# Block-local attention and a three-way maximum layer: transposes moved from TensorE to VectorE and a DRAM scratch, one time table for all engines

## The chip, the core and the metric

The kernel runs on one core of a Trainium2 chip. The core has TensorE (PE, matrix products into PSUM; PEld is its weight load), VectorE (DVE), ScalarE (ACT), GpSimd (POOL) and SyncE (SP), which issues the transfers. Each engine takes its own instructions strictly in order and waits on semaphores for the others. The metric is the device time of one launch in microseconds (us), lower is better.

## The reference

Attention inside chunks of 64 positions, for 8 batches of 8 heads of 576 positions with 64 columns; its output, as 4608 rows of 512, goes through three products with 512x768 weights, their maximum, and one product with a 768x512 weight. All in float32.

```python
scores = scale * np.matmul(q_c, k_c.transpose(0, 1, 2, 4, 3))   # chunks of 64
scores = scores - np.max(scores, axis=-1, keepdims=True)
attn = np.exp(scores)
attn = attn / (np.sum(attn, axis=-1, keepdims=True) + 1e-09)
out = np.matmul(attn, v_c)
x = np.ascontiguousarray(out.transpose(0, 2, 1, 3)).reshape(B * S, H * D)
h = np.maximum(np.maximum(x @ w1, x @ w2), x @ w3)
return (h @ w_out).astype(np.float32)
```

## The kernel before

The 4608 rows are 36 tiles of 128 rows (two chunks of 64 positions, all heads), in nine groups of four tiles.

**Layer.** For a group, `hidden(j, w)` forms one 128x512 piece of x·w1, x·w2 or x·w3 (six `j`, three `w`), and `project` the four output tiles. Every float32 operand is kept as a high part (float32r) and a low part, the rest; `three` adds three products (low·high, high·low, high·high). A group has 72 such threes in `hidden` and 24 in `project`, 96 in all, 24 for each tile.

**Attention.** It makes the x of a later group while the layer of the present group runs. There are two forms. `plain_steps` (tiles below `PLAIN`) multiplies in plain float32, one product per head. `attention` ("stacked") puts high and low part in the two halves of the partitions: `qs` (q), `kk` (k), `vs` (v) and `aa` (the transposed softmax). For a stacked tile TensorE runs: a product of four matmuls for chunk 0 (called s0 here) and chunk 1 (s1), the transposes (`tp`), then the products with v for chunk 0 (x0) and chunk 1 (x1). After each product ACT copies one half out of PSUM and DVE adds the other. After s1 comes the softmax: DVE maximum, POOL subtraction, ACT exponential, DVE sum and reciprocal, POOL multiplication. After the transposes ACT and DVE split the result into `aa`, and two transfers inside SBUF, of 64 partitions each, copy each half of `aa` to the other 64 partitions. After x1, ACT writes the high part `xh` and POOL the low part `xl` of the group's x. The low parts of `qs`, `kk` and `vs` are POOL's too.

**Order.** Up to the eighth tile and the first group's layer the order of all engines is written out by hand (`FIRST`). Behind that only TensorE's order is set by hand: `due` gives each step of a tile a time, and `STEP`, the length of one three, is the clock by which steps are put between the threes. The other engines' instructions are ordered by the framework's scheduler. `now` counts the threes.

The buffers named here (`raw`, `qs`, `kk`, `aa`, `rv`, and the PSUM tiles s, tp and x) exist once each; `pm`, the layer's PSUM tiles, three times.

Of the kernel before, what the change touches and what calls it, by code (L numbers as in the profile page):

```python
# [19 lines left out]
P = 128  # L20
# [5 lines left out]
PLAIN = 10  # L26
# [20 lines left out]
F51f Y63 Y64 B65 A65 P01i F52f C65 hh5f D65 hl5f X65 xl7 H65 Y65p P01z P2z FP01 P3z FP2 FP3  # L47
# [4 lines left out]
def chunk_attn_maxout_kernel(  # L52
# [18 lines left out]
    ep = ctx.enter_context(tc.tile_pool(name="ep", bufs=2))  # L71
# [4 lines left out]
    ao_p = ctx.enter_context(tc.tile_pool(name="ao_p", bufs=1))  # L76
    ps_s = ctx.enter_context(tc.tile_pool(name="ps_s", bufs=1, space=PSUM))
# [88 lines left out]
    def softmax(e):  # L166
        mx = tmp.tile([P, 8], F32, name="mx")
        nc.vector.tensor_reduce(out=mx, in_=e, axis=AX.X, op=ALU.max)
        nc.gpsimd.tensor_tensor(out=e, in0=e, in1=mx.unsqueeze(2).broadcast_to([P, 8, 64]), op=ALU.subtract)
        nc.scalar.activation(out=e, in_=e, func=AF.Exp, scale=SCALE)  # L170
        run(over_sum(e))

    def run(steps):
        for s in steps:
            s()

    def plain_steps(t, x_of, col):
# [23 lines left out]
        def less():  # L201
            st["e"] = ep.tile([P, 8, 64], F32, name="e")
            nc.vector.tensor_tensor(out=st["e"], in0=st["s"],
                                    in1=st["mx"].unsqueeze(2).broadcast_to([P, 8, 64]), op=ALU.subtract)
# [37 lines left out]
    def plain_attention(t, x_of, col):  # L242
        ops = plain_steps(t, x_of, col)
        return [lambda names=names: run(ops[n] for n in names.split())
                for names in ("q v S mx sub exp sum eps rec nrm", "T at", "V xh xl")]

    halves_of = [slice(0, 64), slice(64, 128)]

    def attention(t, x_of, col):

        st = {}

        def stack(hi, src):
            nc.scalar.copy(out=hi, in_=src)  # L256
            nc.gpsimd.tensor_tensor(out=hi[64:], in0=src[64:], in1=hi[64:].bitcast(F32), op=ALU.subtract)  # L257

        def products(pool, name, c, lhs, rhs, out):
            o = pool.tile([P, 4, 2, 2, 64], F32, name=name)  # L260
            for g in range(4):
                nc.tensor.matmul(out=o[:, g].rearrange("p a h x -> p (a h x)"), lhsT=lhs[:, c, g, :],  # L262
                                 rhs=rhs[:, c, g].rearrange("p a x -> p (a x)"), start=True, stop=True)
            for h, rows in enumerate(halves_of):
                nc.scalar.copy(out=out[rows], in_=o[rows, :, 0, h, :])  # L265
            for h, rows in enumerate(halves_of):
                nc.vector.tensor_tensor(out=out[rows], in0=o[rows, :, 1, h, :], in1=out[rows], op=ALU.add)  # L267

        def operands():
            r = att.tile([P, 2, 2, 4, P], F32, name="r", tag="raw", bufs=1)  # L270
            nc.sync.dma_start(out=r, in_=qk2[t - PLAIN])
            rv = att.tile([P, 2, 4, P], F32, name="rv", tag="rv", bufs=1)
            nc.sync.dma_start(out=rv, in_=v2[t - PLAIN])
            qs = att.tile([P, 2, 4, P], F32R, name="qs", tag="qs", bufs=1)
            stack(qs, r[:, 0])
            kk = att.tile([P, 2, 4, 2, P], F32R, name="kk", tag="kk", bufs=1)
            for c in range(2):
                split(kk[:, c, :, 0, :], kk[:, c, :, 1, :], r[:, 1, c], nc.gpsimd)
            st.update(rv=rv, qs=qs, kk=kk)

        def scores(c):
            if c == 0:
                st["e"] = ep.tile([P, 4, 2, 64], F32, name="e")
            products(ps_s, "s", c, st["qs"], st["kk"], st["e"][:, :, c, :])
            if c == 1:
                ef = st["e"].rearrange("p g c k -> p (g c) k")
                softmax(ef)
                vs = st["vs"] = att.tile([P, 2, 4, P], F32R, name="vs", tag=f"vs{t % 2}", bufs=1)
                stack(vs, st["rv"])

        def transpose():
            tp = ps_t.tile([P, 4, P], F32, name="tp")
            for g in range(4):
                nc.tensor.transpose(out=tp[:, g, :], in_=st["e"][:, g].rearrange("p c k -> p (c k)"), identity=ident)  # L294
# [9 lines left out]
        def values(c):  # L304
            if c == 0:
                st["xs"] = xs_p.tile([P, 4, P], F32, name="xs")
            products(ps_x, "x", c, st["vs"], st["aa"], st["xs"][:, :, c * 64:(c + 1) * 64])
            if c == 1:
                xh, xl = x_of()
                split(xh[:, :, col:col + P], xl[:, :, col:col + P], st["xs"], nc.gpsimd)  # L310

        return [operands, lambda: scores(0), lambda: scores(1), transpose, lambda: values(0), lambda: values(1)]
# [3 lines left out]
    def moe(t0, x_of):  # L316
# [5 lines left out]
        def products(j, w, lo, hi):  # L322
            n, cols = hi - lo, slice(lo, hi)
            xh, xl = x_of()
            ps[j, w] = ps_m.tile([P, 512], F32, name="pm")
            for ct in range(CT):
                if ct:
                    yield
                three(ps[j, w][:, :n], wh[j][:, w, ct, :], wl[j][:, w, ct, :], xh[:, ct, cols], xl[:, ct, cols],
                      ct == 0, ct == CT - 1)  # L330

# [18 lines left out]
        def hidden(j, w):  # L350
            yield from products(j, w, 0, 512)
            maximum(j, w, 0, 512)
            if w == 2:
                high(j, 0, 512)
                low(j, 0, 512)

# [12 lines left out]
        def project(*tts):  # L369

            for js in (range(JT - 1), [JT - 1]):
                for tt in tts:
                    for j in js:
                        if (tt, j) != (tts[0], 0):
                            yield
                        onto(tt, j)
                    if JT - 1 in js:
                        output(tt)

        return dict(products=products, maximum=maximum, high=high, low=low, hidden=hidden, onto=onto,  # L380
                    output=output, project=project)

# [6 lines left out]

    def steps_of(i):  # L390
        return [(plain_attention if starts[i] + tt < PLAIN else attention)(starts[i] + tt, lambda: x_tiles(i), tt * P)
                for tt in range(GROUPS[i])]
# [19 lines left out]
    ops["P01i"] = lambda: [g0["onto"](tt, j) for tt in (0, 1) for j in range(JT - 1)]  # L412
    ops["P01z"] = lambda: [g0["onto"](tt, JT - 1) for tt in (0, 1)]
    ops["FP01"] = lambda: [g0["output"](tt) for tt in (0, 1)]
    for tt in (2, 3):
        ops[f"P{tt}z"] = lambda tt=tt: [g0["onto"](tt, j) for j in range(JT)]
        ops[f"FP{tt}"] = lambda tt=tt: g0["output"](tt)

# [20 lines left out]
    STEP = 0.681  # L439
    LENGTH = (3 * JT * CT + 4 * JT) * STEP  # L440

    def due(t):
        g, k = divmod(t, 4)
        if t < PLAIN:
            at = [(k - 4) * 13.0 - 11.0 + d for d in (0.0, 8.0, 13.0)]
        else:
            at = [(k - 4) * LENGTH / 4 - 19.0 + d for d in (-8.0, 0.0, 2.9, 16.5, 25.0, 28.2)]
        return [(g - 1) * LENGTH + a for a in at]

    events = sorted(((at, t, fn) for i in range(2, len(GROUPS)) for tt, u in enumerate(steps_of(i))  # L450
                     for t in [starts[i] + tt] for at, fn in zip(due(t), u)), key=lambda e: e[:2])
    now = 0.0
    with tc.manual_schedule(engines={mybir.EngineType.PE}):
        for i in range(1, len(GROUPS)):
            g = moe(starts[i], lambda i=i: x_tiles(i))
            for part in ([g["hidden"](j, w) for j in range(JT) for w in range(3)]
                         + [g["project"](0, 1), g["project"](2), g["project"](3)]):
                while True:
                    while events and events[0][0] <= now:
                        events.pop(0)[2]()  # L460
                    now += STEP
                    if next(part, part) is part:
                        break
# [41 lines left out]
```

## Time and profile before

| | |
|---|---|
| median of 3 runs | 714.3 us (712.72 to 714.6) |
| the profiled execution | 713.1 us, of which 711.4 us is the span of the instructions |
| TensorE busy | 703.1 us, 99% of the span |
| DVE, ACT, POOL busy | 398.9, 359.8 and 308.9 us |
| transfers | 38.5% of the 16 DMA engines' span, all issued by SP |
| granted TensorE clock | 1.000 |

All rows of the profile and of the trace are of this one execution. A row of the time line gives start, duration, engine, line, operation and tiles (out<-in); an idle stretch before it and who ended it stand in brackets.

### The profile page before, as it was taken

The page shows a single profiled execution, that of the slowest core. Times are in us where ns is not written, and L with a number is a line of the kernel's source. Part 1 is how long each engine was busy: PE and PEld are TensorE (multiplying, and loading weights), DVE is VectorE, ACT ScalarE, POOL GpSimd, SP SyncE. Part 2 cuts the span into 40 slices and gives each one's busy share as a digit, 9 for nine tenths or more (in the row PEclk, how much of TensorE's full clock was granted, in tenths as well). Part 3 has the DMA queues.
Part 4 walks back from the last instruction along what each step waited for, and adds up shares of the span by engine and source line. Part 5 has one row for each costly group of instructions (what it writes and reads, how often), then busy time and mean ns, then how long its engine had stood idle before and what let it go on. Part 6 is the DMA issues. An engine that isn't in the chain of part 4 may idle for free.

```text
span 711.4 us, 9743 instructions
## 1 busy us (share of the span) xinstructions
PE 703.1 (99%) x3545; PEld 592.9 (83%) x3546; DVE 398.9 (56%) x677; ACT 359.8 (51%) x665; POOL 308.9 (43%) x207
## 2 busy tenths in 40 slices
PE   8999999999999999999999999999999999999997
PEld 5997888888888888888888888888888888888886
DVE  7989852456456655676466637664566456521220
ACT  6675551445555555555555555556555655331111
POOL 2443020245656665555665555555566656100000
PEclk9999999999999999999999999999999999999999
DMA  9975640233433354333523363335333541120001
GB/s 365 410 275 185 195 139 31 88 117 114 149 124 119 111 144 131 119 118 84 184 90 118 119 177 119 119 120 171 120 105 107 160 134 33 30 75 15 1 1 59
DMA packets 23215, 90.28 MB, mean 127 GB/s; under 512 B 2944, under 2 KB 2944, under 8 KB 19840
## 3 DMA queue, kind: packets, MB, share of 16 engines
q1 hardware_dynamic: 23168, 89.67, 38.5%
q8 instruction: 28, 0.46, 0.3%
q14 instruction: 19, 0.16, 0.1%
HBM read 66.58 MB, written 9.44 MB: 107 GB/s over the span
## 4 chain that ended last, share of the span: by engine, by line
PE 95%; DMA 2%; DVE 1%; issue 1%; ACT 1%; SPq 0%; POOL 0%; ACTq 0%; DVEq 0%
PE pm L145 27%; PE pm L146 27%; PE pm L147 27%; PE s L262 3%; PE x L262 3%; PE x L227 2%; PE s L194 2%; PE tp L294 2%; DMA buf<-in_w 1%; DMA buf<-in_wout 1%; PE tp L216 1%; ACT ao L117 0%; SPq L108 0%; ACT kk L91 0%; POOL e L162 0%
## 5 line engine op out<-in xcount | busy, mean ns | idle before, releaser
L145 PE MATMUL pm<-xh,wl 128*128 128x512 f32 (+1 forms) x660 | 258.9, 392 | 0.3 <-ACT m L336 0.3
L146 PE MATMUL pm<-xl,wh 128*128 128x512 f32 (+1 forms) x660 | 255.3, 387 | 0.0
L147 PE MATMUL pm<-xh,wh 128*128 128x512 f32 (+1 forms) x660 | 254.9, 386 | 0.0
L147 PEld LDWEIGHTS pm<-xh,wh 128*128 128x128 f32 x660 | 124.1, 188 | 25.8
L145 PEld LDWEIGHTS pm<-xh,wl 128*128 128x128 f32 x660 | 124.4, 188 | 22.7 <-ACT m L336 0.7
L146 PEld LDWEIGHTS pm<-xl,wh 128*128 128x128 f32 x660 | 124.5, 189 | 21.7
L338 DVE TENSOR_TENSOR m<-pm,m 128x512 f32<-128x512 f32 (+1 forms) x110 | 74.9, 681 | 116.1 <-PE pm L147 95.2
L257 POOL TENSOR_TENSOR qs<-r,qs 64x1024 fp32r<-64x1024 f32 x26 | 62.5, 2402 | 148.2 <-ACT qs L256 148.1
L257 POOL TENSOR_TENSOR vs<-rv,vs 64x1024 fp32r<-64x1024 f32 x26 | 62.3, 2397 | 62.5 <-ACT vs L256 62.5
L347 DVE TENSOR_TENSOR hl<-m,hh 128x512 fp32r<-128x512 f32 (+1 forms) x54 | 75.3, 1394 | 17.7 <-ACT hh L344 17.3
L145 PE MATMUL pm<-woh,hl 128*128 128x512 f32 x216 | 85.0, 394 | 0.0
L265 ACT COPY e<-s 64x256 f32<-64x256 f32 x104 | 38.1, 366 | 91.9 <-PE s L262 91.3
L146 PE MATMUL pm<-wol,hh 128*128 128x512 f32 x216 | 84.4, 391 | 0.0
L147 PE MATMUL pm<-woh,hh 128*128 128x512 f32 x216 | 84.2, 390 | 0.0
L267 DVE TENSOR_TENSOR e<-s,e 64x256 f32<-64x256 f32 x104 | 43.8, 421 | 63.6 <-ACT e L265 62.9
L344 ACT CAST hh<-m 128x512 fp32r<-128x512 f32 (+1 forms) x55 | 33.5, 610 | 85.9 <-DVE m L338 85.9
L92 POOL TENSOR_TENSOR kk<-r,kk 128x512 fp32r<-128x512 f32 x52 | 66.7, 1297 | 6.2 <-ACT kk L91 5.7
L267 DVE TENSOR_TENSOR xs<-x,xs 64x256 f32<-64x256 f32 x104 | 43.8, 421 | 30.5 <-ACT xs L265 28.0
L265 ACT COPY xs<-x 64x256 f32<-64x256 f32 x104 | 38.0, 365 | 31.7 <-PE x L262 30.3
L162 POOL TENSOR_TENSOR e<-e,sm 128x512 f32<-128x512 f32 x31 | 32.3, 1043 | 47.0 <-DVE sm L159 43.9
L336 ACT COPY m<-pm 128x512 f32<-128x512 f32 (+1 forms) x55 | 31.8, 579 | 35.6 <-DVE hl L347 22.0
L147 PEld LDWEIGHTS pm<-woh,hh 128*128 128x128 f32 x216 | 40.6, 188 | 8.7
(67 smaller groups left out, 831.4 us busy)
## 6 DMA issues: line engine op xcount, KB each, us to landing
r<-in_qk SPq DMA_DIRECT2D x26, 1024.0 KB, 4.9
rv<-in_v SPq DMA_DIRECT2D x26, 512.0 KB, 3.3
aa<-aa SPq DMA_DIRECT2D x52, 256.0 KB, 3.3
out_x<-ao SPq DMA_DIRECT2D x36, 256.0 KB, 3.6
buf<-in_qk SPq DMA_DIRECT2D x10, 768.0 KB, 7.8
buf<-in_w SPq DMA_DIRECT2D x10, 512.0 KB, 4.5
buf<-in_vb SPq DMA_DIRECT2D x10, 512.0 KB, 6.7
buf<-in_wout SPq DMA_DIRECT2D x6, 512.0 KB, 3.9
```

The source lines that it names most:

```text
L92: eng.tensor_tensor(out=lo, in0=src, in1=hi.bitcast(F32), op=ALU.subtract)
L145: nc.tensor.matmul(out=o, lhsT=al, rhs=bh, start=first, stop=False)
L146: nc.tensor.matmul(out=o, lhsT=ah, rhs=bl, start=False, stop=False)
L147: nc.tensor.matmul(out=o, lhsT=ah, rhs=bh, start=False, stop=last)
L162: eng.tensor_tensor(out=e, in0=e, in1=sm.unsqueeze(2).broadcast_to([P, 8, 64]), op=ALU.mult)
L257: nc.gpsimd.tensor_tensor(out=hi[64:], in0=src[64:], in1=hi[64:].bitcast(F32), op=ALU.subtract)
L262: nc.tensor.matmul(out=o[:, g].rearrange("p a h x -> p (a h x)"), lhsT=lhs[:, c, g, :], rhs=rhs[:, c, g].rearrange("p a x -> p (a x)"), st ...
L265: nc.scalar.copy(out=out[rows], in_=o[rows, :, 0, h, :])
L267: nc.vector.tensor_tensor(out=out[rows], in0=o[rows, :, 1, h, :], in1=out[rows], op=ALU.add)
L338: nc.vector.tensor_tensor(out=banks[j][:, :n], in0=ps[j, w][:, :n], in1=banks[j][:, :n], op=ALU.max)
L344: nc.scalar.copy(out=hh[j][:, lo:hi], in_=banks[j][:, :hi - lo])
L347: eng.tensor_tensor(out=hl[j][:, lo:hi], in0=banks[j][:, :hi - lo], in1=hh[j][:, lo:hi].bitcast(F32), op=ALU.subtract)
```

## The change

Four things are done.

- The four TensorE transposes of a stacked tile go. DVE transposes blocks of 32x32 (`nc.vector.transpose`) of the softmax into a new tile `et`; ACT writes its high part and DVE its low part into `ah` (both operands of that subtraction lie in SBUF); one transfer of 512 KB writes `ah` to a DRAM tile `there`, and two transfers of 512 KB each read it back, each into one half of `aa`'s partitions. The last two wait for the first to land. The two transfers inside SBUF go, and the rows of v are permuted on the host to fit the blocks.
- `PLAIN` falls from 10 to 8: tiles 8 and 9 are stacked too.
- `ep` (the softmax tiles) has one buffer `e` and one `et` in place of two `e`; `ah` takes the place of one of the two `vs`.
- Behind `FIRST` every engine is ordered by hand. A stacked tile's steps have times relative to its s0; the layer's own steps are put in at the end of their product plus 0.3 to 1.8. `STEP` is 0.6815 and `BLOCK`, a product of four matmuls, 0.49. A period of one tile is `total / 4` = 18.3; in the third group the tiles stand 15.9 apart. The first group's `project` is moved from `FIRST` into this table.

```diff
+STEP, BLOCK = 0.6815, 0.49
-PLAIN = 10
+PLAIN = 8
...
-    ep = ctx.enter_context(tc.tile_pool(name="ep", bufs=2))
+    ep = ctx.enter_context(tc.tile_pool(name="ep", bufs=1))
+    dram = ctx.enter_context(tc.tile_pool(name="dram", bufs=2, space=bass.MemoryType.DRAM))
...
+        stack(-8.2, -6.2, "qs", "qs", lambda: st["r"][:, 0])
...
+            products((0.0, 3.3)[c], (1.0, 4.3)[c], ps_s, "s", lambda g, c=c: st["qs"][:, c, g, :],
...
-        def transpose():
-            tp = ps_t.tile([P, 4, P], F32, name="tp")
-            for g in range(4):
-                nc.tensor.transpose(out=tp[:, g, :], in_=st["e"][:, g].rearrange("p c k -> p (c k)"), identity=ident)
-            st["aa"] = aa = att.tile([P, 2, 4, 2, P], F32R, name="aa", tag="aa", bufs=1)
-            for c, rows in enumerate(halves_of):
-                nc.scalar.copy(out=aa[rows, c, :, 0, :], in_=tp[rows])
-            for c, rows in enumerate(halves_of):
-                nc.vector.tensor_tensor(out=aa[rows, c, :, 1, :], in0=tp[rows],
-                                        in1=aa[rows, c, :, 0, :].bitcast(F32), op=ALU.subtract)
-            for c, rows in enumerate(halves_of):
-                nc.sync.dma_start(out=aa[halves_of[1 - c], c].bitcast(F32), in_=aa[rows, c].bitcast(F32))
+        @due(10.3)
+        def _():
+            st["et"] = ep.tile([P, 2, 8, 32], F32, name="et")
+            nc.vector.transpose(out=st["et"], in_=st["e"].rearrange("p g c (k x) -> p k (g c) x", k=2))
+        @due(11.1)
+        def _():
+            st["ah"] = att.tile([P, 2, 2, 8, 32], F32R, name="ah", tag="vs1", bufs=1)
+            nc.scalar.copy(out=st["ah"][:, :, 0], in_=st["et"])
+        @due(11.8)
+        def _():
+            nc.vector.tensor_tensor(out=st["ah"][:, :, 1], in0=st["et"], in1=st["ah"][:, :, 0].bitcast(F32), op=ALU.subtract)
+        @due(12.5)
+        def _():
+            st["there"] = dram.tile([4, 64, 512], F32, name="there")
+            nc.sync.dma_start(out=st["there"].rearrange("n (l k) f -> (n l) k f", k=2),
+                              in_=st["ah"].bitcast(F32).rearrange("p k a n x -> p k (a n x)"))
+        @due(12.9)
+        def _():
+            st["aa"] = att.tile([P, 4, 2, 8, 32], F32R, name="aa", tag="aa", bufs=1)
+            for rows in halves_of:
+                nc.sync.dma_start(out=st["aa"][rows].bitcast(F32).rearrange("p n a g x -> p n (a g x)"),
+                                  in_=st["there"].rearrange("n p f -> p n f"))
...
+            products((21.9, 25.7)[c], (24.3, 27.4)[c], ps_x, "x", lambda g, c=c: st["vs"][:, c, g, :],
...
+        due(28.3)(lambda: nc.scalar.copy(out=x_of()[0][:, :, col:col + P], in_=st["xs"]))
+        @due(29.2)
...
+    total = (3 * JT * CT + 4 * JT) * STEP + 4 * 4 * BLOCK
...
+            first = (i - 1) * total - 32.0 + (tt - 3) * (15.9 if i == 2 else total / 4)
+            for at, pe, fn in attention(starts[i] + tt, lambda i=i: x_tiles(i), tt * P):
+                plan(first + at, pe, fn)
...
+    with tc.manual_schedule(engines={ET.PE, ET.DVE, ET.Activation, ET.Pool, ET.SP}):
```

Three pieces of the instruction order show what that does to the engines, in the middle of the program, in a group's `hidden` part. The number behind a tile's name only tells buffers of one name apart.

ACT before. `xs`, `x` and `xh` belong to a tile t-1, whose last value product (x1) is copied in the first row; `aa` is the next tile t's transposed softmax, `vs` belongs to tile t+1 and `qs` to tile t+2.

```order
L265 COPY xs_3415<-x_3446 64x4x64 x2
L256 CAST vs_3541<-rv_3405 128x1024
L336 COPY m_3463<-pm_3439 128x512
L91 CAST xh_3283<-xs_3415 128x4x128
L265 COPY e_3483<-s_3484 64x4x64 x2
L297 CAST aa_3498<-tp_3493 64x4x128 x2
L265 COPY e_3483<-s_3523 64x4x64 x2
L256 CAST qs_3577<-r_3573 128x1024
```

ACT now. `xs`, `x` and `xh` belong to a tile t-1, `e`, `et` and `ah` to tile t, `qs` and `kk` to tile t+1.

```order
L258 COPY xs_3446<-x_3437 64x4x64 x2
L412 CAST hh_3467<-m_3398 128x512
L323 ACTIVATE e_3411<-e_3411 128x512
L258 COPY xs_3446<-x_3477 64x4x64 x2
L404 COPY m_3489<-pm_3454 128x512
L373 CAST xh_3334<-xs_3446 128x4x128
L270 CAST qs_3505<-r_3442 128x1024
L343 CAST ah_3517<-et_3510 128x2x256
L292 CAST kk_3523<-r_3442 128x4x128 x2
```

The copy of the softmax's high part now stands behind both the `xh` of the tile before and the `qs` of the tile after; before, `qs` stood behind it.

POOL before: the multiplication of tile t's softmax, `vs` of tile t+1, `xl` of tile t-1, `qs` of tile t+2, then the softmax of tile t+1 (`e_3483`) around `kk`.

```order
L162 TENSOR_TENSOR e_3313<-e_3313,sm_3366 128x512
L257 TENSOR_TENSOR vs_3541<-rv_3405,vs_3541 64x1024
L92 TENSOR_TENSOR xl_3284<-xs_3415,xh_3283 128x4x128
L257 TENSOR_TENSOR qs_3577<-r_3573,qs_3577 64x1024
L169 TENSOR_TENSOR e_3483<-e_3483,mx_3532 128x512
L92 TENSOR_TENSOR kk_3580<-r_3573,kk_3580 128x4x128 x2
L162 TENSOR_TENSOR e_3483<-e_3483,sm_3536 128x512
```

POOL now, one period: subtraction of the maximum and multiplication of tile t's softmax, `xl` of tile t-1, `qs` and `kk` of tile t+1, `vs` of tile t.

```order
L318 TENSOR_TENSOR e_3411<-e_3411,mx_3458 128x512
L165 TENSOR_TENSOR e_3411<-e_3411,sm_3485 128x512
L378 TENSOR_TENSOR xl_3335<-xs_3446,xh_3334 128x4x128
L274 TENSOR_TENSOR qs_3505<-r_3442,qs_3505 64x1024
L296 TENSOR_TENSOR kk_3523<-r_3442,kk_3523 128x4x128 x2
L274 TENSOR_TENSOR vs_3551<-rv_3427,vs_3551 64x1024
```

`xl` of the tile before and then `qs` of the tile after now stand directly behind the multiplication by which tile t's softmax is complete; on DVE the subtraction that fills `ah` falls into the same stretch.

SP before: `r` holds q and k and `rv` v of a tile, `aa<-aa` are the two transfers inside SBUF.

```order
L302 DMA aa_3328<-aa_3328 64x1024 x2
L271 DMA r_3573<-in_qk2 128x2048
L273 DMA rv_3575<-in_v2 128x1024
L302 DMA aa_3498<-aa_3498 64x1024 x2
L271 DMA r_3739<-in_qk2 128x2048
L273 DMA rv_3741<-in_v2 128x1024
```

SP now.

```order
L284 DMA rv_3427<-in_v2 128x1024
L279 DMA r_3442<-in_qk2 128x2048
L352 DMA there_3531<-ah_3517 128x1024
L359 DMA aa_3533<-there_3531 64x4x512 x2
L284 DMA rv_3595<-in_v2 128x1024
L279 DMA r_3610<-in_qk2 128x2048
```

The two transfers inside SBUF are replaced by one to DRAM and two back, and the next tile's loads stand behind them in SP's order.

More of the change, by code (lines that the diff above doesn't have):

```diff
@@ L253, in attention @@
         st = {}
[L255 to L260, printed above, removed]
-            for g in range(4):
[L262 to L279, printed above, removed]
@@ L452, in chunk_attn_maxout_kernel @@
[L452 to L463, printed above, removed]
+    total = (3 * JT * CT + 4 * JT) * STEP + 4 * 4 * BLOCK
@@ new lines, in chunk_attn_maxout_kernel @@
+    now = -4 * JT * STEP - 2 * BLOCK
+    with tc.manual_schedule(engines={ET.PE, ET.DVE, ET.Activation, ET.Pool, ET.SP}):
+        for part in parts:
+            for after in part:
+                now += STEP
+                for at, fn in after:
+                    plan(now + at, 0.0, fn)
+                while due and due[0][0] <= now:
+                    _, _, pe, fn = heapq.heappop(due)
+                    fn()
+                    now += pe
+        while due:
+            heapq.heappop(due)[3]()
```

169 lines of the change are left out of this document (103 added, 66 removed).

## The prediction

> **What bounds the kernel now.** I read the page first: the span, the engines' shares, the chain that ended last; then the steady part by a window, and the time line of one tile.
>
> ```profile
> span 711.4 us, 9743 instructions
> PE 703.1 (99%) x3545; PEld 592.9 (83%) x3546; DVE 398.9 (56%) x677; ACT 359.8 (51%) x665; POOL 308.9 (43%) x207
> ...
> PE 95%; DMA 2%; DVE 1%; issue 1%; ACT 1%; SPq 0%; POOL 0%; ACTq 0%; DVEq 0%
> ...
> 500.00:600.00 100.00, 100.00 (x493) 84.57 (x492) 61.98 (x103) 56.28 (x107) 58.83 (x39) 1.00 0.38 116
> ```
>
> TensorE is busy for all of the 100 us window, at full clock, and 95% of the chain is its work. So matmuls taken off it are saved one for one, as long as nothing makes it wait. And a wait of TensorE is paid in full, because there is no idle time in which to lose it. The prediction is therefore two sums: TensorE's work taken away, and TensorE's waits put in. The profiled execution is 713.1 us (711.4 span and 1.7 around it), 1.2 below the median of 714.3; all sums start from 713.1.
>
> **What is taken away.** The price of the four transposes is the start-to-start time they add:
>
> ```profile
> 565.57 0.39 PE L147 MATMUL pm<-woh,hh 128*128 128x512 f32 x1
> 565.80 0.64 PE L262 MATMUL s<-kk,qs 128*128 128x256 f32 x4
> 566.27 0.60 PE L294 MATMUL tp<-ident,e 128*128 128x128 f32 x4
> 566.63 0.48 PE L145 MATMUL pm<-woh,hl 128*128 128x512 f32 x1
> 566.95 0.39 PE L146 MATMUL pm<-wol,hh 128*128 128x512 f32 x1
> ```
>
> Matmuls of the layer start 0.23 apart (565.57 to 565.80), so without the transposes the row at 566.95 would stand at 566.27 + 0.23 = 566.50: they cost 0.45, and a product of four matmuls 0.47 (565.80 to 566.27). 26 tiles x 0.45 = 11.7 us. Tiles 8 and 9 change form; the chain in order of time prices both:
>
> ```profile
> 114.96 1.73 PE s L194 x16
> ...
> 130.69 1.73 PE x L227 x16
> ...
> 162.71 0.47 PE x L262 x4
> ```
>
> Plain is 1.73 + 1.73 and 0.45 of transposes, 3.9; stacked without transposes is 4 x 0.47 = 1.9. Two tiles save 4.1. TensorE's list of waits has one behind `FIRST` that belongs to the change of forms:
>
> ```profile
> PE s L262 <- DVE e L203: 0.8, 1, 0.8
> ```
>
> It is tile 10's product waiting for the plain tile 9 and goes with it. Together 16.6 us: 713.1 - 16.6 = 696.5 if TensorE never waits. The first group's `project` keeps its place in TensorE's order, and `STEP`'s change from 0.681 to 0.6815 only places steps: nothing.
>
> **What waits instead.** The four orders now form a ring. x1 of tile t-1 is copied by ACT, added by DVE, and becomes `xh` on ACT; then ACT casts `qs` of tile t+1 and only then the high part `ah` of tile t; DVE makes `ah`'s low part; the three transfers run; x0 of tile t can start; and x1 of tile t stands five threes behind it. If one turn of the ring is longer than TensorE's work for a tile, TensorE waits for the difference in every tile, however early s0 and s1 come. TensorE's work for a tile is 24 threes and four products: 24 x 0.681 + 4 x 0.47 = 18.2, and 18.3 by the table's 0.49 for a product, which I take, since the matmul behind a product starts a little late. The turn, from rows of the time line:
>
> ```profile
> 560.54 0.64 PE L262 MATMUL x<-aa,vs 128*128 128x256 f32 x4
> 561.21 0.75 ACT L265 COPY xs<-x 64x256 f32<-64x256 f32 x2 [1.24 <-PE x L262]
> 561.99 0.86 DVE L267 TENSOR_TENSOR xs<-x,xs 64x256 f32<-64x256 f32 x2 [1.99 <-ACT xs L265]
> 562.94 0.62 ACT L91 CAST xh<-xs 128x512 fp32r<-128x512 f32 x1
> ...
> 565.64 1.28 POOL L92 TENSOR_TENSOR xl<-xs,xh 128x512 fp32r<-128x512 f32 x1
> ...
> 570.91 1.05 ACT L256 CAST qs<-r 128x1024 fp32r<-128x1024 f32 x1
> 571.87 1.14 ACT L91 CAST kk<-r 128x512 fp32r<-128x512 f32 x2
> ...
> 572.09 2.40 POOL L257 TENSOR_TENSOR qs<-r,qs 64x1024 fp32r<-64x1024 f32 x1 [5.17 <-ACT qs L256]
> ```
>
> - x0 to x1: 0.47 + 5 x 0.681 = 3.88.
> - x1 to the end of `xh`: 560.54 to 563.56 = 3.02.
> - ACT starts the next cast 0.57 behind a 512-column one and 0.96 behind `qs` (570.91 to 571.87). `ah`, 512 columns, so starts 1.53 behind `xh`'s start and ends 1.53 behind its end; DVE could begin the low part at 1.56.
> - At that moment POOL is in the way. It starts 0.13 behind the ACT cast it waits for (571.96 to 572.09). Its order is `xl` (1.28), then `qs` (2.40), so `qs` runs from 1.4 to 3.8 behind `xh`. What DVE then does, the trace shows on the layer's subtraction `hl`, whose operands also both lie in SBUF:
>
> ```profile
> 478.26 2.40 POOL L257 TENSOR_TENSOR qs<-r,qs 64x1024 fp32r<-64x1024 f32 x1 [5.00 <-ACT qs L256]
> ...
> 477.97 0.69 DVE L168 TENSOR_REDUCE mx<-e 128x8 f32<-128x512 f32 x1
> 478.67 2.53 DVE L347 TENSOR_TENSOR hl<-m,hh 128x512 fp32r<-128x512 f32 x1
> ...
> L347 DVE TENSOR_TENSOR hl<-m,hh x54: 417/693/2812, 46.9 to 692.5; 128x512 fp32r<-128x512 f32 x53, 128x256 fp32r<-128x256 f32 x1
> ```
>
> It is 0.69 at the median, but when it meets POOL's `qs` it ends at 481.20, 0.54 behind POOL's end at 480.66. The subtraction that `ah`'s replaces read PSUM. So the low part ends 3.8 + 0.54 = 4.3 behind `xh`. Up to here 3.88 + 3.02 + 4.3 = 11.2.
> - The transfers. No row has a 512 KB store, nor a load from DRAM into 64 partitions.
>
> ```profile
> q1 hardware_dynamic: 23168, 89.67, 38.5%
> ...
> r<-in_qk SPq DMA_DIRECT2D x26, 1024.0 KB, 4.9
> rv<-in_v SPq DMA_DIRECT2D x26, 512.0 KB, 3.3
> aa<-aa SPq DMA_DIRECT2D x52, 256.0 KB, 3.3
> ...
> DMA to landing us min/median/max: 2.0/2.0/2.0
> ...
> 466.90:470.20 3.30, 3.30 (x18) 2.77 (x17) 1.53 (x3) 3.22 (x6) 1.14 (x2) 1.00 0.83 310
> 476.40:477.80 1.40, 1.40 (x8) 1.15 (x7) 1.05 (x3) 1.36 (x3) 0.00 (x0) 1.00 0.97 208
> ```
>
> The 2.0 is the last four output stores, 256 KB, with nothing beside them; 256 KB more at half of what `r` takes over `rv` (1.6) makes 2.8. The two windows lie in the data of one `r` load (128 partitions) and of a first `aa` transfer (64): 310 against 208 GB/s, with the engines 97% busy. The reads go into 64 partitions each, so I take 208: 512 KB in 2.5 us. An `aa` pair (2 x 256 KB) landed 4.1 us behind its first issue (3.3 and the 0.8 between the issues); with 512 KB more, 6.6. With 0.2 for three hand-overs the transfers take 9.6. Bounds: below, the reads at the pace of one `r` load of the same size, 4.9 in place of 6.6; above, two loads from DRAM one after the other, 2 x 3.3 for `rv` and the 2 x 0.85 by which 512 KB at 208 GB/s is slower than at 310, 8.3 (that counts the fixed part twice). The `aa` rows are nearest, because they too fill 64 partitions.
>
> The turn is 11.2 + 9.6 = 20.8, against 18.3 of work: TensorE waits 2.5 us in each tile. The third group's tiles stand 15.9 apart, so its three intervals lose 4.9 each. 28 stacked tiles have 27 intervals: 24 x 2.5 + 3 x 4.9 = 74.7.
>
> **What costs nothing, and under what cover.** The blockwise transpose has no row. The nearest are DVE's 128x512 operations, 0.68 (a reduction) at least, double that at most. It starts behind DVE's addition to `xs`, and `ah` can't start for 1.6 us from there (`xh` and `qs` on ACT), which covers both bounds; without that cover its whole length would enter the turn. The high part is one cast on ACT where there were two. On SP the next `rv` and `r` stand behind the reads, and behind the wait for the write; in the table they stand 7.4 and 9.2 behind the reads (2.0 and -14.5 of the next tiles, against 12.9), and their casts 13.0 and 6.3 behind the loads, more than the 3.3 and 4.9 of their rows; it would cost if the reads ended over 3 us late. Transfers grow from 2.0 to 3.0 MB a tile: the added 1 MB is 5 us at 208 GB/s in a period of 18.3, on engines that are 38.5% busy. `vs` in one buffer, and `e` in one, are read out before they are written again: x1 of a tile is 7 us ahead of the next `vs` cast.
>
> The Trainium skill, "DMA: Bandwidth & Descriptors", section on the anatomy of one DMA, fits 2.0 us + bytes/436 GB/s to a transfer (on GpSimd's path). By it the write takes 3.2, both reads 4.4, and the sum would be near the third rival's. Two 256 KB transfers would take 3.2 by it; the trace has 4.1.
>
> **Rivals.**
> 1. *DVE gets in before POOL's `qs`.* Only some 0.2 us decide it (DVE ready at 1.56, POOL's `qs` from 1.4), and one slower start on POOL would turn it. The low part then ends 1.56 + 0.69 = 2.25 behind `xh`, at 9.15 of a turn of 18.75: 24 x 0.45 + 3 x 2.85 = 19 us of waits, 715.5, about no change. Against it: POOL's queue and ACT's always stand in the same order.
> 2. *Nothing waits; faster.* Both the meeting with POOL and the half-rate reads must be absent: turn 9.15 + 7.9 = 17.05, below 18.3. It decides from 18.3 on. The time is 696.5, and perhaps 0.1 a tile more where x1 waits for DVE's addition of x0, which now stands behind the softmax's maximum and one of the layer's: 699. For it: the `aa` rows are SBUF to SBUF, and the limit could lie on the reading side.
> 3. *The reads run at full rate, POOL still blocks DVE.* Turn 11.2 + 7.9 = 19.1: 24 x 0.8 + 3 x 3.2 = 29 us, 725, slower.
>
> **How the numbers follow.** The likeliest case is the full ring, 696.5 + 74.7 = 771; its own range is 750 to 792, from 0.8 us less or more a turn (27 x 0.8 = 22), half of the way to either bound of the reads. Chances: 0.48 for it, 0.18 for the first rival, 0.24 for the second, 0.10 for the third. A difference under 0.3% (2.1 us) can't be told from none. Faster is 0.24 and a third of the first rival, 0.30. Same is half of the first rival, 0.10 with a little of the third. Slower 0.60. The range runs from 697 to 784: a tenth lies below, in the second rival, and a tenth above, where the reads are near their upper bound.
>
> **What would show it.** TensorE's list of waits should be headed by x waiting for the landing of `aa<-there`, 27 times about 2.5 us, the longest in the third group. The transpose should take 0.7 to 1.4; `ah<-et,ah` on DVE 2 to 3 us with POOL's `qs` over it; the write to DRAM 2.8 and the second read 6 to 7 from the first's issue. TensorE's busy time should fall by the 16 us whatever comes. If `ah` takes 0.7 on DVE the first rival holds; if the second read lands within 5 us of the first's issue and `ah` still takes 2 to 3, the third; if there is no PE wait for `aa`, the second. The prediction fails if the ring isn't closed: if ACT makes `ah` before x1 of the tile before is done.

## The result, and the profile after

The changed kernel takes 803.5 us (median of 4 runs, 800.9 to 806.0) against 713.6 for the kernel before on the same chip: a ratio of 1.126 (95% interval 1.122 to 1.130), slower, and further than the forecast of 771 and the end of its range at 784. The profiled execution is 800.9 us, 799.0 of it span. First the page of the changed kernel: busy time by engine, the chain by engine, and the chain by line cut to what it names first.

```profile
span 799.0 us, 9517 instructions
PE 717.1 (90%) x3402; PEld 594.5 (74%) x3402; DVE 436.0 (55%) x693; ACT 352.5 (44%) x663; POOL 339.6 (42%) x219
...
PE 45%; DMA 30%; DVE 12%; ACT 6%; issue 3%; SPq 2%; POOL 0%; DVEq 0%; ACTq 0%; POOLq 0%
```

TensorE, 99% busy before, now stands idle for 81.9 us (799.0 - 717.1), and the chain runs through transfers for 30% of the span. Yet its busy time has risen by 14.0 us, with 143 instructions fewer. These are two losses. The list of TensorE's waits of the changed kernel (total, times, longest) shows the first:

```profile
PE x L252 <- DMA aa<-there: 71.9, 25, 4.5
```

The second is the clock. Here is the window of 500 to 600 us, whose row of before was all busy at a clock of 1.00 (the number ahead of the DMA share):

```profile
500.00:600.00 100.00, 88.46 (x397) 73.19 (x396) 56.45 (x86) 45.91 (x88) 49.23 (x31) 0.95 0.46 146
```

One turn of the ring, in the changed kernel's chain in order of time (start, length, what), from x0 of a tile to x0 of the next and on to its x1. A piece of the chain begins where the one before it ends, so x1 itself starts 0.16 ahead of its piece (at 437.38):

```profile
433.38 0.71 PE x L252 x4
...
437.54 0.49 PE x L252 x4
...
441.85 2.91 DVE ah L347
444.78 2.60 DMA there<-ah
...
447.46 0.58 SPq L359
...
448.08 6.62 DMA aa<-there
...
454.79 0.71 PE x L252 x4
...
457.15 0.43 PE pm L150
...
460.54 0.48 PE x L252 x4
```

The turn is 21.4 us (433.38 to 454.79), and the chain has no link in it that the prediction's ring had not. In the next tile the piece of x1 comes 5.75 us behind x0, not 4.16 as in the first (437.54 - 433.38), since matmuls of the layer take 0.43 us there, twice the usual 0.23. So turns alternate: x0 starts at 389.03, 410.53, 433.38, 454.79, 477.80 and 499.37 in the same chain, 21.5, 22.9, 21.4, 23.0 and 21.6 apart. The clock's records of this run have 14 stretches of 3.41 us at half clock between 152 and 705 us. Eleven of them, from 234 to 678 us, come 44.4 us apart, in every second tile.

### The profile page after: what moved, and what is told of

The parts are those of the page before. It is cut to its first block, busy times and chain, and to the rows that moved or that the text cites. A ratio compares the mean times of both kernels' runs of the same rounds, so it can differ in the third digit from the quotient of the medians.

```text
span 799.0 us, 9517 instructions
## 1 busy us (share of the span) xinstructions
PE 717.1 (90%) x3402; PEld 594.5 (74%) x3402; DVE 436.0 (55%) x693; ACT 352.5 (44%) x663; POOL 339.6 (42%) x219
## 4 chain that ended last, share of the span: by engine, by line
PE 45%; DMA 30%; DVE 12%; ACT 6%; issue 3%; SPq 2%; POOL 0%; DVEq 0%; ACTq 0%; POOLq 0%
DMA aa<-there 20%; PE pm L148 12%; PE pm L149 12%; PE pm L150 12%; DVE ah L347 8%; DMA there<-ah 8%; PE x L252 4%; ACT qs L270 2%; DVE xs L263 2%; SPq L359 2%; ACT xs L258 2%; PE x L219 2%; DMA buf<-in_wout 1%; PE s L186 1%; ACT ah L343 1%
## 5 line engine op out<-in xcount | busy, mean ns | idle before, releaser
L148 PE MATMUL pm<-xh,wl 128*128 128x512 f32 (+1 forms) x660 | 262.2, 397 | 0.0
L150 PE MATMUL pm<-xh,wh 128*128 128x512 f32 (+1 forms) x660 | 260.5, 395 | 0.0
L149 PE MATMUL pm<-xl,wh 128*128 128x512 f32 (+1 forms) x660 | 260.2, 394 | 0.0
L149 PEld LDWEIGHTS pm<-xl,wh 128*128 128x128 f32 x660 | 127.7, 193 | 23.9
L406 DVE TENSOR_TENSOR m<-pm,m 128x512 f32<-128x512 f32 (+1 forms) x110 | 74.7, 679 | 89.2 <-PE pm L150 79.5
L263 DVE TENSOR_TENSOR e<-s,e 64x256 f32<-64x256 f32 x112 | 47.3, 422 | 124.6 <-ACT e L258 123.9
L252 PE MATMUL x<-aa,vs 128*128 128x256 f32 x224 | 38.4, 294 | 75.2 <-DMA aa<-there 71.9
L252 PEld LDWEIGHTS x<-aa,vs 128*128 128x128 f32 x224 | 32.2, 189 | 83.9 <-issue 79.3
L318 POOL TENSOR_TENSOR e<-e,mx 128x512 f32<-128x512 f32 x28 | 29.7, 1061 | 129.3 <-DVE mx L314 129.3
L296 POOL TENSOR_TENSOR kk<-r,kk 128x512 fp32r<-128x512 f32 x56 | 80.9, 1464 | 2.1
L347 DVE TENSOR_TENSOR ah<-et,ah 128x512 fp32r<-128x512 f32 x28 | 72.3, 2583 | 14.9 <-ACT ah L343 14.9
L274 POOL TENSOR_TENSOR qs<-r,qs 64x1024 fp32r<-64x1024 f32 x28 | 67.2, 2401 | 28.8 <-DMA buf<-in_wout 26.6
```

The lines of the kernel that those rows point to most:

```text
L148: nc.tensor.matmul(out=o, lhsT=al, rhs=bh, start=first, stop=False)
L149: nc.tensor.matmul(out=o, lhsT=ah, rhs=bl, start=False, stop=False)
L150: nc.tensor.matmul(out=o, lhsT=ah, rhs=bh, start=False, stop=last)
L263: nc.vector.tensor_tensor(out=out()[rows], in0=st[name][rows, :, 1, h, :], in1=out()[rows], op=ALU.add)
L274: nc.gpsimd.tensor_tensor(out=st[name][64:], in0=src()[64:], in1=st[name][64:].bitcast(F32), op=ALU.subtract)
L296: nc.gpsimd.tensor_tensor(out=st["kk"][:, c, :, 1, :], in0=st["r"][:, 1, c], in1=st["kk"][:, c, :, 0, :].bitcast(F32), op=ALU.subtract)
```

## The experiments

The kernel before took 714.0 to 714.6 us (medians) beside these runs; each ratio is against it on the same chip.

**POOL makes `kk`'s first low part ahead of `qs`'s.** It moves the meeting on DVE's way and leaves the rest.

```
-        stack(-8.2, -6.2, "qs", "qs", lambda: st["r"][:, 0])
+        stack(-8.2, -3.3, "qs", "qs", lambda: st["r"][:, 0])
```

> POOL makes the low part of kk's first chunk before that of qs; ACT's order stays. kk's first cast stands behind ah on ACT, so POOL is idle when DVE is ready for ah's low part. Ring with the port meeting as a part of it: ah's subtraction on DVE falls from 2.9 to 0.7 us, a turn from 21.3 to about 19.2, TensorE's waits for aa from 72 to about 33 us in all (24 x 1.0 and three of about 3.3), the half clock goes because no wait reaches 2.7 us outside the third group, and the time is about 730 us. If the meeting is beside the ring (the transfers or ACT alone set it): 803 as before. If kk comes too late instead: waits of s0 for POOL of up to 0.5 us a tile, up to 745.

732.3 us, ratio 1.025 (1.024 to 1.027). The operations on `ah` in this kernel's trace (instructions, then min, median and max in ns), with those of the changed kernel ahead of them in a fence of their own:

```profile
L347 DVE TENSOR_TENSOR ah<-et,ah x28: 693/2901/2924, 119.4 to 710.6; 128x512 fp32r<-128x512 f32 x28
```

```profile
L347 DVE TENSOR_TENSOR ah<-et,ah x28: 691/693/2845, 120.0 to 641.2; 128x512 fp32r<-128x512 f32 x28
```

The same subtraction takes 0.69 when POOL's `qs` isn't running over it, so the 2.2 us are those of the meeting with POOL, as the prediction took from `hl`. The turn in the chain is 19.2 (x0 at 401.87 and 497.91, five turns). The time falls by 71 us, some 60 of which are 2.2 us in 27 turns; the rest fits the clock, at a mean of 0.995 here against 0.970, though no run shows that part by itself.

**ACT makes `ah` ahead of the `qs` cast.** One due time, and the meeting goes by another way.

```
-        stack(-8.2, -6.2, "qs", "qs", lambda: st["r"][:, 0])
+        stack(-7.0, -6.2, "qs", "qs", lambda: st["r"][:, 0])
```

> ACT makes ah's high part before it casts qs of the next tile; all else stays. Ring: ah ends 1.0 us earlier, and DVE is then ready while POOL is in xl, not yet in qs, so it waits for the end of xl alone: ah's low part ends about 2.0 us behind xh's end in place of 4.4, a turn is about 19.0, the time about 723 us (24 x 0.7 and three of 3.1 of waits on 696.5), with the clock at full. If only ACT's 1.0 us counts and DVE still meets qs: the turn falls by less than 0.2, 800. If the ring isn't what sets the waits: 803.

725.9 us, ratio 1.017 (1.015 to 1.019). The subtraction has a median of 0.77, and three turns take 56.9 (x0 at 417.99 and 474.84), 18.95 each. Here `ah` has left the ring of the tile before: in 15 tiles it waits for its own tile's transpose, 5.5 us in all. Both edits move one instruction of one engine, and either takes 2.2 to 2.5 us out of a turn of 21.4, so the ring is what set the pace.

**A fill for TensorE's wait.** Eleven unused products into a PSUM tile ahead of each x0, so that TensorE works while it waits; the output doesn't change.

```
+                if name == "x" and at < 22.0:
+                    tp = ps_t.tile([P, 512], F32, name="tp")
+                    for _ in range(11):
+                        nc.tensor.matmul(out=tp, lhsT=wh[0][:, 0, 0, :], ...)
```

> Eleven products that nobody reads (2.5 us) stand on TensorE before each x0, so that it works where it waited; nothing else changes. If the waiting itself makes the granted clock fall to half: the fourteen stretches of 3.4 us at half clock go, every turn is about 21.2 where every second one was 23, and the time falls by about 12 x 1.75 = 21 us to about 782, though TensorE has 70 us of matmuls more. If the half clock comes from the amount of work or from something outside: it stays or grows, 803 or more. If x0's start and not the clock set the long turns: 803.

785.6 us, ratio 1.100 (1.098 to 1.102): more work on TensorE and 18 us less than the changed kernel. Its window of 500 to 600 us:

```profile
500.00:600.00 100.00, 98.37 (x464) 81.14 (x463) 58.32 (x84) 45.08 (x87) 54.48 (x34) 1.00 0.51 159
```

No stretch of half clock is left in the part with stacked tiles, and every turn is 21.5 (x0 at 406.36, 427.91, 449.42, 470.86 and 492.36). So the clock falls because TensorE waits, and those 18 us are its price. TensorE still waits 0.2 to 0.8 us in most tiles, and no half clock follows.

**Five unused products in place of eleven** leave a pause of about 1.6 us a tile (`range(11)` becomes `range(5)`).

> The changed kernel with 5 unused products ahead of each x0 in place of the 11 of the earlier experiment: about 1.1 us of the wait is filled, and TensorE still stands still for some 1.6 to 1.8 us in every tile. In the runs so far pauses of up to 1.9 us were never followed by a stretch of half clock, and those from 1.9 to 3.0 us in part. Theory (the clock falls by the length of the pause, with a limit near 1.9 us): the granted clock stays above 0.995 and the time is that of the 11 products, 783 to 787 us. Rival (any regular wait of more than 1 us lowers the clock, in proportion to the time idle): a clock near 0.985 and 792 to 797 us.

787.8 us, ratio 1.103 (1.102 to 1.105), mean clock 0.989. The time lies 0.8 us above what the theory named and 4 us short of the rival's; the clock lies between the two, nearer the rival's, and over half of what it lost was lost ahead of 200 us. Behind 200 us two stretches of half clock came, among 23 pauses. The first of the two followed a pause of 1.80 us (ahead of x0 at 448.54), while pauses of 2.04 and 2.12 us (ahead of 405.65 and 514.91) had none behind them. The windows below lie on the grid that the clock's records show in this run: a window of 3.41 us, and the one behind it, two such pairs.

```profile
445.27:448.68 3.41, 1.61 (x9) 1.07 (x8) 1.53 (x3) 1.09 (x3) 0.55 (x1) 1.00 1.05 262
448.68:452.09 3.41, 3.41 (x11) 2.83 (x12) 0.84 (x3) 1.85 (x4) 0.49 (x1) 0.50 0.94 390
489.64:493.05 3.41, 1.67 (x11) 1.13 (x9) 1.53 (x3) 0.73 (x2) 0.38 (x1) 1.00 1.06 262
493.05:496.46 3.41, 3.41 (x17) 2.89 (x18) 1.93 (x4) 1.89 (x4) 0.66 (x1) 1.00 0.79 327
```

With TensorE busy for 1.61 of the 3.41 us the next window is at half clock, with 1.67 it is at full. So the length of the pause alone didn't decide, as my theory had it; the last section takes this up.

**Reads into all 128 partitions.** Each of the two reads fetches half of the pieces for all partitions; the rows of `aa` then stand in another order than the products need.

```
-            for rows in halves_of:
-                nc.sync.dma_start(out=st["aa"][rows]..., in_=st["there"].rearrange("n p f -> p n f"))
+            wide = st["there"].rearrange("n p f -> (n p) f").rearrange("(m p) f -> p m f", m=2)
+            for m in range(2):
+                nc.sync.dma_start(out=st["aa"][:, 2 * m:2 * m + 2]..., in_=wide)
```

> Each of the two reads from DRAM goes to all 128 partitions for two of the four 2 KB pieces, in place of 64 partitions for all four; bytes, pieces and number of transfers are the same. The rows of aa are thereby put in a wrong order (the output isn't the reference's). If 64 partitions halve the rate: the reads fall from 7.3 us (first issue to second landing) to about 5.2, a turn from 21.3 to 19.2, the time to about 728 with the clock at full. If the reads are slow for another reason (they follow a write, 2 KB pieces, the issue on SP): they stay at 7 and the time at 803.

743.9 us, ratio 1.039 (1.035 to 1.044). Issue to landing of one read (min, median, max), first in the changed kernel, then here:

```profile
DMA to landing us min/median/max: 4.6/5.7/6.8
```

```profile
DMA to landing us min/median/max: 3.6/4.7/5.5
```

In the chain the first read is issued at 399.72 and the second has landed at 405.21, 5.5 us, against 7.2 in the turn above (447.46 to 454.70): 1.7 less, which is what stood between the prediction's two prices, 6.6 and 4.9. So two reads that each fill 64 partitions do run at the lower pace. The time is longer than the expected 728 because the reads fell by 1.7 and not by 2.1: 21.4 - 1.7 = 19.7, as x0 at 385.64 and 405.34 shows, where 19.2 was expected, and the two turns with a stretch of half clock exceed 21.

**The kernel before with two plain tiles fewer** (`PLAIN = 10` becomes 8), to price the change of form alone.

> The kernel before with tiles 8 and 9 stacked like those behind them, and nothing else of the change. It prices the term of 4.9 us that the prediction gave to these tiles (3.9 us of TensorE's products and 0.8 us of tile 10's wait). By the prediction's rows: 709 us, 0.993 of the kernel before. Rival (the two tiles' stacked work on the other engines makes TensorE wait as much as it saves): 714 us, 1.00.

721.3 us, ratio 1.010 (1.009 to 1.012): slower, not 0.7% faster. The waits that are new in its list:

```profile
PE s L262 <- POOL kk L92: 5.7, 1, 5.7
PE tp L294 <- POOL e L162: 3.7, 1, 3.7
```

Four of POOL's operations, from a `vs` at 111.67 to the subtraction at 118.53, now stand one behind the other at the first stacked tile, while POOL did nothing between 102.5 and 120.7 in the kernel before. The trace has 31 matmuls fewer, but the first stacked tile costs more than they bring: TensorE waits 9.4 us, and four windows of 3.41 us at half clock follow.

**The ring cut.** A new table: `ah` ahead of `qs` on ACT, `qs` last among POOL's low parts, the load of `r` earlier, x0 and x1 1.7 to 1.8 us later with what follows. The edits stand in the order of the code: the load of `r`, the stacking of `qs`, the casts and the low parts of `kk`, the x products, `xh`, `xl`, and where a tile's table starts.

```
-        @due(-14.5)
+        @due(-21.8)
...
-        stack(-8.2, -6.2, "qs", "qs", lambda: st["r"][:, 0])
+        stack(-7.1, -6.2, "qs", "qs", lambda: st["r"][:, 0])
...
-            @due(-6.6 + 0.6 * c)
+            @due((-9.4, -6.1)[c])
...
-            @due(-4.0 + 1.3 * c)
+            @due((-9.0, -3.8)[c])
...
-            products((21.9, 25.7)[c], (24.3, 27.4)[c], ps_x, "x", ...
+            products((23.6, 27.5)[c], (24.4, 30.3)[c], ps_x, "x", ...
...
-        due(28.3)(lambda: nc.scalar.copy(out=x_of()[0][:, :, col:col + P], in_=st["xs"]))
+        due(31.2)(lambda: nc.scalar.copy(out=x_of()[0][:, :, col:col + P], in_=st["xs"]))
...
-        @due(29.2)
+        @due(33.4)
...
-            first = (i - 1) * total - 32.0 + (tt - 3) * (15.9 if i == 2 else total / 4)
+            first = (i - 1) * total - 36.0 + (tt - 3) * (15.2 if i == 2 else total / 4)
```

> The changed kernel with a new time table: the ring is cut. The load of the q and k rows is due 7.3 us earlier, ScalarE's cast of qs comes behind that of ah, POOL's qs low part is the last of its set, POOL's low part of kk chunk 0 is early, and TensorE's two groups of x products stand 1.7 to 1.8 us later, with what follows from them. Theory (the loss is the ring: x0 to x1, xh, ah, the write and the reads, which a turn of 18.3 us has no room for; the granted clock falls only as a consequence of TensorE's waits): the ring shortens by about 3.3 us at ah (2.9 to 0.7 for the subtraction, 1.0 for the cast ahead) and gains 1.7 us of room by the later products, so that TensorE waits in few tiles or none: 697 to 708 us at a clock of 1.0, TensorE's idle time under 20 us. Rival (the transfers through the scratch or the clock are slow by themselves, whatever the order): the time stays over 720 us, with waits for the reads at x in most tiles.

719.5 us, ratio 1.008 (1.007 to 1.009). Behind 200 us TensorE is 98 to 99% busy at full clock, so the ring is gone; the expected 697 to 708 was missed by two waits at the start. One of them in the chain of this kernel:

```profile
119.70 0.34 SPq L279
...
120.85 7.26 DMA there<-ah
...
128.85 6.35 DMA aa<-there
...
135.33 1.19 PE x L252 x4
```

The earlier load (line 279, 1 MB) is issued 1.15 us ahead of the write in the third group, whose tiles stand closer, and with a store of 256 KB between them, and the write takes 7.26 us in place of 2.60.

**The load behind the reads.**

```
-        @due(-21.8)
+        @due({10: -17.3, 11: -17.3, 12: -20.3}.get(t, -21.8))
```

> The cut ring with one more edit: for tiles 10, 11 and 12 the load of the q and k rows is due 1.5 to 4.5 us later, so that it is issued behind the two reads of the tile before and not ahead of that tile's write. In the trace of the cut ring TensorE waited 6.4 and 4.9 us at x in the third group, where this load (1 MB) was issued 1.2 and 0.9 us ahead of the write, and the write took 7.3 and 6.4 us in place of 2.6; each wait was followed by a stretch of half clock. Theory (the write stands behind the load's bytes): the writes there take 2.6 to 3 us, both waits and both stretches of half clock go, 11.3 + 3.4 us: 703 to 707 us, 0.985 to 0.990 of the kernel before, at a clock of 1.0. Rival (the third group has no room for the transfers of a tile in 15.2 us, whatever their order): the waits move to the load's own users or to the next tile, and the time stays at 714 to 720 us.

717.9 us, ratio 1.005 (1.004 to 1.007). The writes take 2.6 again, so the theory was right about the write; but the rival was right about the time. The load now lands at 132.0, and TensorE waits 6.6 us for DVE's additions, which stand behind what the late load holds up.

**The v rows later, the table 0.8 us earlier.**

```
-        @due(2.0)
+        @due(8.0 if t in (9, 10, 11) else 2.0)
-            first = (i - 1) * total - 36.0 + ...
+            first = (i - 1) * total - 36.8 + ...
```

> The cut ring with the later load of the q and k rows, and two more edits: for tiles 9, 10 and 11 the load of the v rows is due 6.0 us later, so that it does not share the queue with the load of the q and k rows just ahead of it, and the whole table of the stacked tiles stands 0.8 us earlier (POOL's xl was 0.6 us late for TensorE five times). In the trace of the kernel before this edit both loads were issued within 0.7 us and landed 8.1 and 8.7 us later; alone they take 4.8 and 3.5 us; ScalarE's and VectorE's casts behind the late one carried the wait to x. Theory (the third group's transfers fit when each lands before the next is issued): the load of the q and k rows lands 5 to 6 us after its issue, TensorE's waits in the third group fall from 8.0 us to under 3 us and no stretch of half clock is left: 703 to 709 us, 0.985 to 0.993 of the kernel before. Rival (15.2 us a tile are too few for the work of the third group, whatever the order of the loads): the waits stay at 6 us or more in the third group, 714 to 718 us.

713.6 us, ratio 0.9989 (0.9980 to 0.9999): as fast as before. The load of the v rows hardly moved: in the first of the three tiles SP still issued it 0.65 us behind that of the q and k rows (124.41 and 125.06), for a due time is only a place in SP's order, and nothing ahead of it there waits. The gain is in the steady part, where TensorE no longer waits from 300 to 600 us. The third group still waits 12.2 us, where under 3 were expected, and its time line names the place:

```profile
124.41 0.54 SPq L279 DMA_DIRECT2D r<-in_qk  x1
...
132.23 0.62 ACT L292 CAST kk<-r 128x512 fp32r<-128x512 f32 x1 [7.68 <-DMA r<-in_qk]
...
133.35 0.64 ACT L323 ACTIVATE e<-e 128x512 f32<-128x512 f32 x1
```

ACT stands for 7.68 us at the cast of the next tile's `kk`, with the exp of this tile, which would lead to the next write, behind it.

**The casts behind the exp.**

```
-        st = {}
+        st, late = {}, t in (10, 11, 12)
-        stack(-7.1, -6.2, "qs", ...)
+        stack(-3.9 if late else -7.1, -3.6 if late else -6.2, "qs", ...)
-            @due((-9.4, -6.1)[c])
+            @due(((-6.6, -4.0) if late else (-9.4, -6.1))[c])
-            @due((-9.0, -3.8)[c])
+            @due(((-5.9, -3.7) if late else (-9.0, -3.8))[c])
```

> The kernel before this one (cut ring, loads behind the reads, table 0.8 us earlier) with one more edit: for tiles 10, 11 and 12 the casts of kk and qs and POOL's low parts stand 2.8 to 5.3 us later in the order, behind ScalarE's exp of the tile before (and behind its ah, for all but the first). In that kernel's trace TensorE's remaining waits all lie at 120 to 190 us, 12.2 us with about 3 us of half clock, and the chain there runs through ScalarE: its cast of kk waits for the load of the q and k rows that lands at 132.2, with the exp of the tile before, 5 us long ready, queued behind it. Theory (a wait in one engine's order that holds the ring of another tile): the exp no longer stands behind the load, the write of tile 9 is issued some 5 us earlier, and most of the third group's waits go: 701 to 707 us, 0.982 to 0.990 of the kernel before. Rival (the load itself is too late for its own tile, whoever is queued behind it): TensorE waits at s instead of x, as long in all: 711 to 716 us.

706.3 us, ratio 0.989 (0.987 to 0.990): 1.1% faster than the kernel before. The exp ran at 126.53, 6.8 us earlier, and the write of tile 9 was issued at 135.05, 5.6 us earlier. The page and the window of this kernel:

```profile
PE 691.2 (98%) x3401; PEld 578.6 (82%) x3402; DVE 375.1 (53%) x693; ACT 355.2 (51%) x663; POOL 322.8 (46%) x219
...
500.00:600.00 100.00, 100.00 (x480) 83.94 (x479) 54.19 (x102) 55.21 (x104) 60.15 (x40) 1.00 0.57 181
```

So the change's idea holds on this chip: with the same operations and transfers, the change is worth 8 us once the order leaves room for the round trip.

## Why the prediction was wrong, point by point

- *TensorE's work taken away, 15.8 us without tile 10's wait.* Right, within some 2 us. In the last kernel TensorE is busy for 691.2 us; 703.1 - 15.8 = 687.3, and 1.7 for its one stretch of half clock in the tiles makes 689.0. The 0.8 of tile 10's wait and the 4.1 of tiles 8 and 9 don't come by themselves: in the kernel before, the earlier change of form cost 9.4 us of new waits.
- *The ring, and what closes it.* Right from the fourth group on. The 25 waits for the landing of `aa<-there` head the list, and two edits of one due time each shortened the turn by what they took away. In the third group it is another ring: its tiles stand 15.9 apart, and with that spacing the due times put `ah` (11.1) ahead of the `xh` of the tile before (28.3 - 15.9 = 12.4), so that the step through `xh` falls out. ACT's rows of the changed kernel show it:

```profile
139.16 0.62 ACT L343 CAST ah<-et 128x512 fp32r<-128x512 f32 x1 [1.48 <-DVE et L338]
...
140.29 0.62 ACT L373 CAST xh<-xs 128x512 fp32r<-128x512 f32 x1
```

The three intervals there cost 4.5, 1.0 and 1.6 us of waiting (ahead of x0 at 151.57, 170.67 and 188.43), 7.1 in all, and not 3 x 4.9 = 14.7. The 23 waits behind them are 2.9 on average, 66.4 in all, against 60 for 24 forecast. So it is luck that all the waits at x together, 75.1, come so near to the 74.7 of the sum.
- *x0 to x1, 3.88.* 4.00 at full clock, start to start (433.38 to 437.38). The matmul behind an x0 that had waited starts 0.55 behind it (433.93), not 0.47; in the fill's kernel, behind waits of a few tenths, it is 0.56 (427.91 to 428.47).
- *x1 to `ah`'s low part, 3.02 + 4.3.* 7.38 (437.38 to 444.76) against 7.32: right to 0.1, the meeting of DVE with POOL's `qs` included, 2.91 for the subtraction. The transpose, 0.71, was covered.
- *The transfers, 9.6.* 10.0: the write 2.6 (2.8 forecast), the reads 7.2 from the first's issue to the second's landing (6.6). The choice of the half-partition pace was right. The Trainium skill's fit ("DMA: Bandwidth & Descriptors", the section on the anatomy of one DMA) gave an estimate of 3.2 for the write; the trace has 2.6.
- *The turn, 20.8.* 21.4 at full clock, 0.6 more, mostly the transfers' 0.4. In the fill's kernel the 23 turns behind the third group make that some 15 us, of which the third group's three turns give 3 back (59.3 us from 132.63 to 191.95, against 62.4). That kernel shows what the forecast was worth without the clock: 785.6 against 771, inside the 750 to 792 that the likeliest case had of its own, and 1.6 beyond the end of the range at 784.
- *TensorE's work at full clock: the step that failed.* The prediction priced every matmul at the 1.00 that the rows of before show, and wrote that TensorE's busy time falls by 16 us "whatever comes". It rose by 14.0: 14 stretches of 3.41 us at half clock lose 23.9 us of work; each of 27 pauses adds 0.24, because the last matmul ahead of it counts 0.39 to its end and not 0.23 to the next start, and the first product behind it is 0.08 longer, 6.5 in all; and - 15.8 + 23.9 + 6.5 = 14.6. TensorE's idle time grew by 73.6 us (8.3 to 81.9), as much as the prediction's waits (by the luck named above), so in TensorE's own account nearly all of the miss is here. Because a stretch mostly lies between x0 and x1, it lengthens the ring too, by 1.6 us in every second turn; taken away, it was worth 18 us (803.5 to 785.6). The 32.5 between 771 and 803.5 are these 18 and the 14.6 by which the fill's kernel misses the forecast.
- *The rivals.* DVE did not get in ahead of POOL's `qs`, and no read of the changed kernel ran at the full pace. Where an edit brought the first rival about (POOL's `kk` first), the time was 732.3 and not 715.5: the turn was 19.2 and not 18.75, which is 12 of the 17 us; up to 3.4 of the other 5 are two stretches of half clock, at 133 and 153 us, and the rest stays open.

## What to carry to other kernels

Moving work off the bounding engine onto a longer path is worth its time only if the path, from the engine and back to it, is shorter than the engine's work for a turn; write that loop down with every queue it passes, then break it by order alone, which here was worth 97 us with the same operations. TensorE may also lose its clock when it waits regularly, so price a wait of a few us a tile at more than its length. And a due time in a table is only a place in a queue: look for what is queued behind a waiting instruction, and for which transfer was issued just ahead of the one that matters.

## What the runs showed of the hardware

The half clock follows a fixed grid. In each run the clock's records begin on a multiple of 3.41 us from one another, and what decided was TensorE's idle time within one window of that grid. Over the ten kernels here that have such stretches behind the start, and up to TensorE's last instruction, windows at full clock were followed by half clock 32 times, each after 1.80 us or more idle in the window (53%), and about 2,000 times they were not, each with 1.76 us or less; the ends of matmuls are modelled, so the limit itself is good to perhaps 0.1 us. One window at the start does not fit: in the kernel with five unused products, that of 11.77 to 15.18 us had only 1.10 us idle, and half clock followed; why stays open. A window that is at half clock already stayed there with less, 0.8 to 1.3 us, three times. The changed kernel shows why only every second tile was hit, in windows of its own grid, two with one wait between them and two a turn later:

```profile
428.65:432.06 3.41, 2.01 (x11) 1.55 (x9) 1.78 (x5) 0.73 (x2) 0.07 (x1) 1.00 1.10 241
432.06:435.47 3.41, 2.09 (x11) 1.86 (x12) 1.59 (x4) 0.73 (x2) 1.04 (x1) 1.00 1.02 380
452.55:455.96 3.41, 1.17 (x7) 1.11 (x8) 1.53 (x3) 0.57 (x2) 1.05 (x1) 1.00 1.05 309
455.96:459.37 3.41, 3.41 (x10) 2.64 (x9) 1.91 (x5) 1.49 (x4) 0.58 (x1) 0.50 0.88 365
```

The first wait is cut by the grid's edge into 1.40 and 1.32 us idle, and nothing happens; the second has 2.24 us in one window, and the next is at half clock. That stretch makes the turn 1.6 us longer, two turns come to 13 windows (44.4 us), and the pattern holds itself from 234 to 678 us. The Trainium skill, "TensorE: Matmul & The Clock Gate", section "What's actually happening", has the free-running window of 3.4 us, which these records bear out; it puts the half clock behind a whole idle window, and here 1.8 us of one was enough.

Two more numbers: a transfer of 512 KB to DRAM, 2.60 us by itself, took 7.26 with a load of 1 MB issued 1.15 us ahead of it on the same queue and a store of 256 KB between; and a VectorE subtraction of 128x512 with both operands in SBUF went from 0.69 to 2.91 us when it began as POOL's `qs`, 2.40 us long, did.
